# Moving an fp32 gather behind its P V, and one P V behind two score sums, in a decode attention kernel

## Chip, cores, metric

One core of a Trainium2 chip. The metric is the device time of one execution in microseconds (us), the median of several runs. The span of a profiled execution is about 1.8 us shorter than its device time.

## The reference

The kernel computes one decode step of a gated mix of two blocks, for a batch of 8.

```python
# A: cached attention. x [8,1,576], k_cache and v_cache [8,32,4096,128] bf16
q = (x @ wq).reshape(8, 1, 32, 128).transpose(0, 2, 1, 3)
p = softmax(einsum("bhqd,bhkd->bhqk", q, k_cache) * 128**-0.5)
a = einsum("bhqk,bhkd->bhqd", p, v_cache).transpose(0, 2, 1, 3).reshape(8, 1, 4096) @ wo
# B: an MLP of width 4608 on layernorm(x)
b = gelu(layernorm(x) @ w1 + b1) @ w2 + b2
g = sigmoid((x * gate_w).sum(-1, keepdims=True))
out = g * a + (1 - g) * b
```

The K and V caches are 537 MB of the 557 MB that have to be read. There is one query per head, so nothing is read twice.

## The kernel before

The work is cut into 64 groups (`NG`), each of 4 heads of one batch element: 4 MiB of K and 4 MiB of V. K and V have two buffers each. One group passes through these steps:

1. `mult`: VectorE multiplies a quarter of K by the broadcast q (bf16).
2. Sum: TensorE adds the products up, 8 matmuls with the identity.
3. `reduce`: VectorE adds the remaining 16 columns. Steps 1 to 3 run four times per group, c = 0 to 3.
4. `softmax`: the maximum on VectorE, the exponentials on ScalarE.
5. `pv`: P V on TensorE, 32 matmuls. Their result is 128x512 and holds the wanted rows in pieces.
6. `evict`: ScalarE copies it to `O_sb` (fp32, a single buffer).
7. `gather`: TensorE picks and adds the pieces, 4 fp32 matmuls, which the trace records as 8 passes.
8. `norm`: VectorE divides by the row sums, which `total` has summed over partitions.

P V of group g-1 runs within group g. All engines work from queues in the order of recording, so the place of a call in this loop is its place on TensorE. Cuts are marked "[...]".

```python
def scores(g, between):
    mult(g, 0); between(0)          # mult(g, c) also records sum c on TensorE
    mult(g, 1); between(1)
    for c in range(NCK):            # NCK = 4
        reduce(g, c)
        if c + 2 < NCK:
            mult(g, c + 2); between(c + 2)

def evict(g):    # ScalarE: O_sb <- PSUM; waits for pv(g) and for the gather of g-1
def gather(g):
    for tt in range(TQ):            # TQ = 4
        p_oz[g] = op("tensor", lambda e, tt=tt: e.matmul(
            oz_ps[:, 0:HB], lhsT=O_sb[:, tt, :], rhs=sel16[:, tt, :], start=(tt == 0), stop=(tt == TQ - 1)),
            [a_ev[g], v_norm.get(g - 1), c_sel16] if tt == 0 else ())

V_LAST = (32, 32, 16, 16, 16, 8, 8)  # load_v_pieces: the last V comes in 7 pieces of the 128 tiles
                                     # and waits, as every load_v(g), for pv(g-2), which frees its buffer
for g in range(NG):
    [...]  # load_k(g + 1), load_v(g)
    def between(c, g=g):
        if c == 0 and 2 <= g < NG - 1:
            gather(g - 2)                    # between sum 0 and sum 1
        if c == 1 and g >= 1:
            rowsum(g - 1)
            if g < NG - 1:
                if g >= 2:
                    norm(g - 2)
                total(g - 1)
        [...]  # c == 2: portions of the MLP and of the output projection
        if c == 3:
            if 1 <= g < NG - 2:
                pv(g - 1, 0, 1)
                evict(g - 1)
            if g == NG - 1:
                gather(NG - 3)
            [...]
    scores(g, between)
    [...]  # g == NG - 3: load_k(g + 2), load_v(g)
    if g + 1 < NG:
        q_of(g + 1)                          # broadcast the next q
    [...]
    softmax(g)
    if g == NG - 2:
        pv(g - 1, 0, 1)                      # P V of 61, before the sums of group 63
        evict(g - 1)
        load_v_pieces(g + 1)
last = NG - 1
norm(last - 2); pv(last - 1, 0, 1); evict(last - 1); total(last - 1); rowsum(last)
pv_turned(last, (0,))      # the last P V is turned: V is the stationary operand, 128 small matmuls
gather(last - 1); norm(last - 1)
pv_turned(last, (1,)); total(last); recip(last)
pv_turned(last, range(2, len(V_LAST))); norm_turned(last)
[...]  # the last part of the output projection, the mix with g, and the stores
```

## Time and profile before

1312.12 us, median of 3 runs (1311.38 to 1313.95).

These are lines of the page of the kernel before: the busy time of each engine with its share of the span (PE is TensorE at a matmul, PEld TensorE loading weights, DVE VectorE, ACT ScalarE, POOL GpSimd), and, in 40 equal slices of the span, the busy tenths of the DMA engines and what they moved.

```profile
span 1310.0 us, 12641 instructions
PE 870.3 (66%) x5428; PEld 416.0 (32%) x5428; DVE 870.8 (66%) x1061; ACT 204.1 (16%) x393; POOL 2.5 (0%) x13
...
DMA  9999999999999999999999999999999999999997
GB/s 401 418 432 431 432 431 431 432 432 432 432 429 431 430 430 432 425 417 432 432 431 432 430 432 431 432 430 432 431 429 431 430 432 431 431 432 432 431 418 295
```

No compute engine is busy for more than two thirds of the span, but the DMA engines are at work in all slices but the last, at about 431 GB/s. The Trainium skill, "DMA: Bandwidth & Descriptors" (Bandwidth), gives 435 GB/s as the ceiling of the fabric; the trace agrees to within 1%.

The view of waits (engine, line and tile, "<-" what it waited for, total us, times, longest) says how much slack the compute has:

```profile
DVE p L354 <- DMA KB<-in_A_k_cache_dram: 182.4, 62, 14.8
...
DVE rz L438 <- PE psb L432: 123.8, 62, 2.4
DVE s_sb L369 <- PE psb L364: 105.0, 90, 3.3
```

VectorE (DVE, line 354 is `mult`) waits 182.4 us for K, 2.9 us per group. Line 438 is the reciprocal in `norm`; it waits 2 us in each group for the gather (line 432). As there is slack in each group, that wait alone doesn't say that it costs time.

The timeline of the last 30 us (start, length, engine, line, what, count, and in brackets how long the engine sat idle before and what ended that) tells another story. L414 is P V, L364 the sums, L187 the issue of the last V, L396 the exponentials, L508 the turned P V:

```profile
1281.20 4.45 DVE L354 TENSOR_TENSOR p<-KB,q_bc 128x4096 bf16<-128x4096 bf16 x2
1284.28 3.35 PE L414 MATMUL psb<-VB,P 128*16 128x512 bf16 x32 [4.93 <-DMA VB<-in_A_v_cache_dram]
...
1287.56 3.63 PE L364 MATMUL psb<-p,ident 128*128 128x512 bf16 x16
1287.68 4.04 SPq L187 DMA_DIRECT2D VB<-in_A_v_cache_dram  x7
...
1299.16 2.34 ACT L396 ACTIVATE P<-s_sb,mD 32x128 bf16<-32x128 f32 x4 [10.88 <-DVE mD L393]
...
1301.64 0.94 PE L508 MATMUL psb<-P,VB 128*128 128x4 bf16 x32 [1.56 <-ACT P L396]
1302.45 1.03 PE L432 MATMUL psb<-sel,O_sb 128*128 128x4 f32 x8
...
1304.44 1.85 PE L508 MATMUL psb<-P,VB 128*128 128x4 bf16 x64
```

The products of group 63 are under way from 1281.20, but their sums wait on TensorE behind P V of group 61, whose V lands only at 1284.24. Once started, nothing on TensorE waits for a DMA any more: the last line has no bracket. The end of this kernel is compute.

### The profile page before, as it was taken

The page shows a single profiled execution, that of the slowest core. Times are in us where ns is not written, and L with a number is a line of the kernel's source. Part 1 is how long each engine was busy: PE and PEld are TensorE (multiplying, and loading weights), DVE is VectorE, ACT ScalarE, POOL GpSimd, SP SyncE. Part 2 cuts the span into 40 slices and gives each one's busy share as a digit, 9 for nine tenths or more (in the row PEclk, how much of TensorE's full clock was granted, in tenths as well). Part 3 has the DMA queues.
Part 4 walks back from the last instruction along what each step waited for, and adds up shares of the span by engine and source line. Part 5 has one row for each costly group of instructions (what it writes and reads, how often), then busy time and mean ns, then how long its engine had stood idle before and what let it go on. Part 6 is the DMA issues. An engine that isn't in the chain of part 4 may idle for free.

```text
span 1310.0 us, 12641 instructions
## 1 busy us (share of the span) xinstructions
PE 870.3 (66%) x5428; PEld 416.0 (32%) x5428; DVE 870.8 (66%) x1061; ACT 204.1 (16%) x393; POOL 2.5 (0%) x13
## 2 busy tenths in 40 slices
PE   3466877776647676646765855766765756766756
PEld 1133433443313333323332322333332322332323
DVE  4576676666647677647766666767676676666675
ACT  1201011111110110101011011111011011111111
POOL 0000000000000000000000000000000000000000
PEclk8778777868776888768878788878878787878888
DMA  9999999999999999999999999999999999999997
GB/s 401 418 432 431 432 431 431 432 432 432 432 429 431 430 430 432 425 417 432 432 431 432 430 432 431 432 430 432 431 429 431 430 432 431 431 432 432 431 418 295
DMA packets 25256, 557.78 MB, mean 426 GB/s; under 512 B 2529, under 2 KB 6641, under 8 KB 7537
## 3 DMA queue, kind: packets, MB, share of 16 engines
q1 hardware_dynamic: 24944, 556.95, 99.3%
q8 instruction: 42, 0.69, 0.2%
q14 instruction: 14, 0.11, 0.0%
q10 hardware_dynamic: 256, 0.03, 0.0%
HBM read 556.96 MB, written 0.01 MB: 425 GB/s over the span
## 4 chain that ended last, share of the span: by engine, by line
DMA 66%; DVE 17%; PE 16%; issue 0%; ACT 0%; SPq 0%
DMA KB<-in_A_k_cache_dram 64%; DVE p L354 14%; PE psb L364 12%; PE psb L432 3%; DVE s_sb L369 3%; DMA VB<-in_A_v_cache_dram 2%; PE psb L414 0%; PE psb L508 0%; DVE rz L438 0%; DVE OT_sb L439 0%; ACT P L396 0%; ACT L467 0%; SPq L187 0%; SPq L223 0%; PE psb L477 0%
## 5 line engine op out<-in xcount | busy, mean ns | idle before, releaser
L364 PE MATMUL psb<-p,ident 128*128 128x512 bf16 x2048 | 638.9, 469 | 415.7 <-DVE p L354 415.7
L354 DVE TENSOR_TENSOR p<-KB,q_bc 128x4096 bf16<-128x4096 bf16 x256 | 579.6, 2285 | 182.4 <-DMA KB<-in_A_k_cache_dram 182.4
L364 PEld LDWEIGHTS psb<-p,ident 128*128 128x128 bf16 x2048 | 223.5, 119 | 723.5 <-DVE p L354 449.9
L369 DVE TENSOR_REDUCE s_sb<-psb 128x32 f32<-128x512 f32 x256 | 175.7, 687 | 105.3 <-PE psb L364 105.0
L427 ACT ACTIVATE O_sb<-psb 128x512 f32<-128x512 f32 x63 | 37.6, 597 | 1030.2 <-PE psb L414 1030.2
L396 ACT ACTIVATE P<-s_sb,mD 32x128 bf16<-32x128 f32 x256 | 147.0, 574 | 18.2 <-DVE mD L393 14.4
L414 PE MATMUL psb<-VB,P 128*16 128x512 bf16 x2016 | 121.4, 383 | 4.9 <-DMA VB<-in_A_v_cache_dram 4.9
L432 PEld LDWEIGHTS psb<-sel,O_sb 128*128 128x128 f32 x504 | 99.7, 274 | 21.0 <-issue 16.2
L438 DVE RECIPROCAL rz<-psb 128x4 f32<-128x4 f32 x63 | 11.5, 182 | 123.8 <-PE psb L432 123.8
L432 PE MATMUL psb<-sel,O_sb 128*128 128x4 f32 x504 | 86.3, 294 | 0.0
L414 PEld LDWEIGHTS psb<-VB,P 128*16 128x16 bf16 x2016 | 45.0, 89 | 75.7 <-issue 27.5
L402 DVE TENSOR_REDUCE rs<-P 128x4 f32<-128x512 bf16 x64 | 43.5, 680 | 2.1 <-ACT P L396 2.1
L421 PEld LDWEIGHTS psb<-rs,ones 128*128 128x128 f32 x128 | 30.7, 241 | 15.3 <-issue 8.0
L348 ACT ACTIVATE q_bc<-psb 128x128 bf16<-128x128 f32 x64 | 17.4, 271 | 32.4 <-PE psb L346 32.4
L421 PE MATMUL psb<-rs,ones 128*128 128x4 f32 x128 | 20.9, 234 | 0.0
L452 PEld LDWEIGHTS psb<-yT_sb,RB 128*128 128x128 bf16 (+1 forms) x216 | 19.4, 165 | 3.4
L452 PE MATMUL psb<-yT_sb,RB 128*128 128x8 bf16 (+1 forms) x216 | 19.8, 227 | 0.0
L387 DVE TENSOR_REDUCE mA<-s_sb 128x1 f32<-128x128 f32 x64 | 18.3, 286 | 2.2
L389 DVE STREAM_TRANSPOSE mB<-mA 128x32 f32<-128x32 f32 x64 | 13.6, 212 | 2.2
L393 DVE STREAM_TRANSPOSE mD<-mC 128x32 f32<-128x32 f32 x64 | 13.5, 211 | 2.2
L346 PEld LDWEIGHTS psb<-Q,Sel 128*128 128x128 bf16 x64 | 6.1, 96 | 27.4 <-issue 27.2
L346 PE MATMUL psb<-Q,Sel 128*128 128x128 bf16 x64 | 14.7, 230 | 0.0
(63 smaller groups left out, 85.5 us busy)
## 6 DMA issues: line engine op xcount, KB each, us to landing
KB<-in_A_k_cache_dram SPq DMA_DIRECT2D x64, 4096.0 KB, 26.0
VB<-in_A_v_cache_dram SPq DMA_DIRECT2D x63, 4096.0 KB, 31.8
RB<-in_B_w_dram SPq DMA_DIRECT2D x1, 5184.0 KB, 43.7
RB<-in_B_w_dram SPq DMA_DIRECT2D x1, 4608.0 KB, 35.8
RB<-in_A_wo_dram SPq DMA_DIRECT2D x1, 4608.0 KB, 43.8
RB<-in_A_wq_dram SPq DMA_DIRECT2D x1, 4096.0 KB, 12.5
VB<-in_A_v_cache_dram SPq DMA_DIRECT2D x2, 1024.0 KB, 10.3
VB<-in_A_v_cache_dram SPq DMA_DIRECT2D x3, 512.0 KB, 12.9
```

Source lines behind the costliest of these rows:

```text
L346: t = op("tensor", lambda e: e.matmul(qb_ps[:, 0:DH], lhsT=Sel[:, b, :], rhs=Q4[:, hg * DH:(hg + 1) * DH], start=True, stop=True), [a_Q[hg ...
L354: v_mult[g, c] = op("vector", lambda e: e.tensor_tensor(out=p1[:, par, :, :], in0=KB[s][:, c * CT:(c + 1) * CT, :], in1=qb, op=ALU.mult), ...
L364: p_sum[g, c] = op("tensor", lambda e, r=r, n=n: e.matmul(tr_ps[par][:, :], lhsT=ident[:, :], rhs=r, start=(n == 0), stop=(n == NCH - 1)), w)
L369: v_red[g, c] = op("vector", lambda e: e.tensor_reduce(out=s_sb[:, s, c * CT:(c + 1) * CT], in_=tr_ps[par][:, :].rearrange("p (t c) -> p t ...
L387: t = op("vector", lambda e: e.tensor_reduce(out=mA[:, 0:1], in_=s_sb[:, s, :], axis=AX.X, op=ALU.max), [v_red[g, NCK - 1], c_mA])
L396: a_exp[g] = op("scalar", lambda e, h=h, q=q: e.activation(out=P[q, s, :, h], in_=s_sb[q, s, :], func=ACT.Exp, bias=mD[q, s, 0:1], scale=1.0),
L402: v_rs[g] = op("vector", lambda e: e.tensor_reduce(out=rs[:, s, :], in_=P[:, s, :, :].rearrange("p t h -> p h t"), axis=AX.X, op=ALU.add), ...
L414: p_pv[g] = op("tensor", lambda e, o=o, tq=tq: e.matmul(o, lhsT=P[:, s, tq * TQ:(tq + 1) * TQ, :].rearrange("p t h -> p (t h)"), rhs=VB[s] ...
L421: p_z[g] = op("tensor", lambda e: e.matmul(oz_ps[:, HB:2 * HB], lhsT=ones[:, :], rhs=rs[:, g % 2, :], start=True, stop=True), [v_rs[g], v_ ...
L427: a_ev[g] = op("scalar", lambda e: e.activation(out=O_sb[:].rearrange("p t d -> p (t d)"), in_=o_ps[s][:, :], func=ACT.Copy), [p_pv[g], p_ ...
L432: p_oz[g] = op("tensor", lambda e, tt=tt: e.matmul(oz_ps[:, 0:HB], lhsT=O_sb[:, tt, :], rhs=sel16[:, tt, :], start=(tt == 0), stop=(tt == ...
L452: st["p_up"] = op("tensor", lambda e, w=w, o=o, kt=kt: e.matmul(o, lhsT=w, rhs=yT_sb[:, kt, :], start=(kt == 0), stop=(kt >= NKF)), [*ld_w ...
```

## The change

The intent is to take the gather out of the chain of a group's sums. It is put where TensorE idles, behind P V and the next q broadcast. In the last group, P V of 61 is put behind the first two sums, so that they don't wait for its V.

```diff
         def between(c, g=g):
-            if c == 0 and 2 <= g < NG - 1:
-                gather(g - 2)
             if c == 1 and g >= 1:
                 rowsum(g - 1)
                 if g < NG - 1:
                     if g >= 2:
                         norm(g - 2)
                     total(g - 1)
+                else:
+                    pv(NG - 3, 0, 1)
+                    evict(NG - 3)
+                    load_v_pieces(g)
[...]
-                if g == NG - 1:
-                    gather(NG - 3)
[...]
             load_wo()
+        if 1 <= g < NG - 2:
+            gather(g - 1)
+        if g == NG - 1:
+            gather(g - 2)
         softmax(g)
-        if g == NG - 2:
-            pv(g - 1, 0, 1)
-            evict(g - 1)
-            load_v_pieces(g + 1)
     last = NG - 1
```

## The prediction

> **What bounds the kernel.** The page: span 1310.0 us, TensorE and VectorE each 66% busy, but the DMA row is 9 in 39 of 40 slices, at about 431 GB/s. The chain of waits is 66% DMA, nearly all landings of K. The Trainium skill, "DMA: Bandwidth & Descriptors" (Bandwidth), gives a fabric ceiling of 435 GB/s; this trace sits at it. In the group view VectorE waits 182.4 us for K over 62 groups: about 3 us of slack in each.
>
> Each load raises its semaphore 16 times, once per DMA engine (same page, why a DMA increments by 16). In the trace's semaphore records the last of the 16 moves by 9.71 us per 4 MiB, from 24.7 to 1304.39 us almost without a break; the first engines run up to 8.2 us ahead of it. So the slowest engine is the clock, from the first K to the last piece of V at 1304.39; then a tail of 5.6 us.
>
> **What the change does.** Nothing is added or removed; only TensorE's order moves.
> 1. The gather (4 fp32 matmuls, 8 passes, 0.8 to 1.7 us in the timeline) leaves the place between sums 0 and 1 and stands behind the next q broadcast, where TensorE idles 5 us. There it waits about 0.7 us for the eviction (0.60 us). Sums, the reciprocal that waited for it (123.8 us in all) and the first score reduction come about 1.1 us earlier per group. All of this becomes more waiting for K: gain in steady state 0.
> 2. Group 62 (VectorE-bound behind its K at 1264.8) ends about 1.05 us earlier, so group 63 starts near 1280.15, not 1281.20.
> 3. In group 63 P V of 61 (3.35 us at half clock, 1284.28 to 1287.63) no longer stands before the sums. Sum 0 starts near 1282.5 instead of 1287.56; the group's exponentials end near 1298.2 (1301.5 before).
> 4. The price: the last V's pieces wait for that P V, which now follows two sums and ends near 1289.8, so they are issued 2.2 us later (1287.68 before). Before, the first engines idled about 2.5 us for them (V of 62 landed there at 1287.86, the first piece at 1292.80), but the slowest engine had work until 1294.43 and received the first piece 2.49 us later, without a gap. Now the first engines receive it near 1295, the slowest still at about 1296.9. Last landing stays near 1304.4 (estimate from these times).
>
> **The critical path.** Before, the end was compute: the last 64 turned P V matmuls ran 1304.44 to 1306.29 without waiting, then 3.7 us to the end. After, they wait for the last piece: 1304.4 + 0.1 + 8 tiles at 29 ns = 1304.8, plus 3.7 = 1308.4. Gain about 1.5 us: 0.1%.
>
> **Predicted:** 1310.7 us (1312.12 - 1.5), 80% range 1308.8 to 1312.9. Faster by over 2%: 0.5%; within 2%: 98.5%; slower: 1%.
>
> **What would show it.** VectorE's wait for K grows from 182 to about 240 us; the reciprocal's wait for the gather falls from 124 to nearly 0; gathers sit 0.7 us behind the q broadcast; the last V is issued near 1289.8; the DMA dip at 1287 to 1290 is longer; the chain ends with a landing of V ahead of the last turned P V.
>
> **What would make it wrong.** P V of 61 later than about 1292: the slowest engine starves and the end slips by as much. The late issue costing all 16 engines alike: the end 1 to 2 us later, the gain gone. One more 1.2 us hiccup of the slowest engine. A run-to-run level (before: 1311.38 to 1313.95) that shifts as much as the effect.

## The result

1310.72 us, median of 4 runs (1310.44 to 1311.21); the kernel before, in all its runs up to then, 1313.03 us (1311.38 to 1314.13). The ratio is 0.9984, 95% interval 0.9967 to 1.0001. A ratio here is the mean time of one kernel's runs over the mean of the other's of the same rounds, so not quite the ratio of the medians. The interval touches 1; what speaks for a real gain is that all runs of the changed kernel lie close together and the profile shows where the time went.

The same lines of the page after:

```profile
span 1308.8 us, 12641 instructions
PE 843.5 (64%) x5428; PEld 384.4 (29%) x5428; DVE 869.7 (66%) x1061; ACT 204.1 (16%) x393; POOL 2.5 (0%) x13
...
DMA  9999999999999999999999999999999999999997
GB/s 398 422 431 432 431 432 431 432 431 430 434 424 432 430 431 429 428 418 432 429 431 429 431 431 431 431 432 430 432 430 431 431 431 429 432 431 432 429 420 311
```

And of the waits after:

```profile
DVE p L354 <- DMA KB<-in_A_k_cache_dram: 278.0, 62, 16.0
...
DVE s_sb L369 <- PE psb L364: 129.6, 127, 1.9
...
PE psb L432 <- ACT O_sb L427: 32.9, 61, 0.5
...
DVE rz L438 <- PE psb L432: 1.9, 1, 1.9
```

The wait of the reciprocal for the gather has gone (123.8 to 1.9 us) and the wait for K has grown by 95.6 us, 1.5 us per group. The rate of the DMA did not move. So the time that the gather's new place takes out of each group's chain turned into more waiting for K. The gather itself now waits 0.5 us for the eviction, where TensorE had nothing else to do.

The timeline after of the same stretch:

```profile
1280.30 4.45 DVE L354 TENSOR_TENSOR p<-KB,q_bc 128x4096 bf16<-128x4096 bf16 x2
...
1282.60 5.05 PE L364 MATMUL psb<-p,ident 128*128 128x512 bf16 x16 [4.15 <-DVE p L354]
...
1287.58 1.90 PE L414 MATMUL psb<-VB,P 128*16 128x512 bf16 x32
...
1289.53 3.77 SPq L187 DMA_DIRECT2D VB<-in_A_v_cache_dram  x7
...
1295.62 2.34 ACT L396 ACTIVATE P<-s_sb,mD 32x128 bf16<-32x128 f32 x4 [5.49 <-DVE mD L393]
...
1298.91 1.62 PE L432 MATMUL psb<-sel,O_sb 128*128 128x4 f32 x8
...
1303.47 1.00 PE L508 MATMUL psb<-P,VB 128*128 128x4 bf16 x24 [0.63 <-DMA VB<-in_A_v_cache_dram]
1304.72 0.38 PE L508 MATMUL psb<-P,VB 128*128 128x4 bf16 x8 [0.25 <-DMA VB<-in_A_v_cache_dram]
```

The exponentials of group 63 start 3.54 us earlier (1295.62, not 1299.16). The last V is issued 1.85 us later (1289.53, not 1287.68). The last turned P V now carries a bracket: it waits for the last pieces of V. Of the 3.5 us won, 1.2 us reach the end of the span.

Why did the later issue not cost more? A load raises its semaphore once for each of the 16 DMA engines that carry it, as the Trainium skill, "DMA: Bandwidth & Descriptors" (Why a DMA increments its semaphore by 16 and not by 1), says; the trace has the 16 times. Here are the first and the last of the 16, in us, read from the semaphore records of both traces:

```
                          before: first engine, last     after: first engine, last
V of group 61                     1278.15  1284.24              1277.87  1284.17
V of group 62                     1287.86  1294.43              1287.58  1294.68
V of group 63, issued at          1287.68                       1289.53
  piece 1 (1 MiB)                 1292.80  1296.92              1294.24  1297.14
  piece 7 (256 KB)                1300.77  1304.39              1302.09  1304.68
```

The engines are far apart. The first one had landed V of 62 by 1287.86 before and 1287.58 after, and landed piece 1 only 4.9 and 6.7 us later. Moving a piece takes about 2.5 us, as the last engine shows, so the first one stood idle for about 2.5 us before and 4.2 us after (an estimate from these times). The last engine was still at work on V of 62 and went on with piece 1 without a gap: it landed it 2.49 us later before and 2.46 us later after. These last landings set the end of the changed kernel. They come 0.3 us later than before, but 0.25 us of that is there already at V of 62, on an engine that did not have to wait for the late issue. (In a second trace of the changed kernel V of 62 is no later than before, at 1294.39, and the time is lost at piece 6, which lands 0.98 us after piece 5, not 0.62. A later section shows what costs such time.) The delay hit engines that had time. (The records do not name the engine of a landing; that the last one is the same engine from load to load is read from the even steps of the last landing.)

### The profile page after: what moved, and what is told of

The parts are those of the page before. It is cut to its first block, busy times and chain, and to the rows that moved or that the text cites. A ratio compares the mean times of both kernels' runs of the same rounds, so it can differ in the third digit from the quotient of the medians.

```text
span 1308.8 us, 12641 instructions
## 1 busy us (share of the span) xinstructions
PE 843.5 (64%) x5428; PEld 384.4 (29%) x5428; DVE 869.7 (66%) x1061; ACT 204.1 (16%) x393; POOL 2.5 (0%) x13
## 4 chain that ended last, share of the span: by engine, by line
DMA 69%; DVE 20%; PE 10%; SPq 0%; issue 0%; ACT 0%
DMA KB<-in_A_k_cache_dram 68%; DVE p L354 16%; PE psb L364 10%; DVE s_sb L369 3%; DMA VB<-in_A_v_cache_dram 1%; SPq L187 0%; PE psb L414 0%; ACT L467 0%; SPq L229 0%; DVE mA L387 0%; SPq L223 0%; PE psb L477 0%; DVE mB L389 0%; ACT O_sb L427 0%; DVE gm L390 0%
## 5 line engine op out<-in xcount | busy, mean ns | idle before, releaser
L364 PE MATMUL psb<-p,ident 128*128 128x512 bf16 x2048 | 610.9, 459 | 412.2 <-DVE p L354 411.8
L354 DVE TENSOR_TENSOR p<-KB,q_bc 128x4096 bf16<-128x4096 bf16 x256 | 579.6, 2285 | 278.0 <-DMA KB<-in_A_k_cache_dram 278.0
L364 PEld LDWEIGHTS psb<-p,ident 128*128 128x128 bf16 x2048 | 218.1, 114 | 744.5 <-DVE p L354 445.2
L432 PE MATMUL psb<-sel,O_sb 128*128 128x4 f32 x504 | 66.9, 256 | 32.9 <-ACT O_sb L427 32.9
L432 PEld LDWEIGHTS psb<-sel,O_sb 128*128 128x128 f32 x504 | 61.6, 192 | 41.3 <-ACT O_sb L427 41.2
L421 PEld LDWEIGHTS psb<-rs,ones 128*128 128x128 f32 x128 | 24.4, 192 | 9.3 <-issue 0.4
L390 DVE TENSOR_REDUCE gm<-mB 128x1 f32<-128x32 f32 x64 | 11.9, 186 | 2.2
```

The source lines that it names most:

```text
L354: v_mult[g, c] = op("vector", lambda e: e.tensor_tensor(out=p1[:, par, :, :], in0=KB[s][:, c * CT:(c + 1) * CT, :], in1=qb, op=ALU.mult), ...
L364: p_sum[g, c] = op("tensor", lambda e, r=r, n=n: e.matmul(tr_ps[par][:, :], lhsT=ident[:, :], rhs=r, start=(n == 0), stop=(n == NCH - 1)), w)
L421: p_z[g] = op("tensor", lambda e: e.matmul(oz_ps[:, HB:2 * HB], lhsT=ones[:, :], rhs=rs[:, g % 2, :], start=True, stop=True), [v_rs[g], v_ ...
L432: p_oz[g] = op("tensor", lambda e, tt=tt: e.matmul(oz_ps[:, 0:HB], lhsT=O_sb[:, tt, :], rhs=sel16[:, tt, :], start=(tt == 0), stop=(tt == ...
```

## The experiments

Twelve kernels ran, each beside the kernel before on the same chip. One interval of ratios is 0.0025 wide or wider, more than most of the effects looked for, so the verdicts rest on spans and times in the traces, and the ratios are given with them.

### The changed kernel again

No edit.

> The changed kernel once more, as the yardstick of this chip. Theory T (the gain is in the tail alone: compute of group 63 comes forward by about 3.5 us and the end is then set by the last landing of V): ratio 0.9985 to 0.9995, span near 1308.8. Rival S (the gather's place gives the time in all groups): the same, so this run does not tell them apart.

Measured: 1310.74 us (1310.59 to 1311.04, 5 runs), before on this chip 1311.91 (1310.37 to 1314.81, 9 runs), ratio 0.9990 (0.9977 to 1.0002); span 1308.9. The last landing was at 1304.75. The result repeats. The runs of the kernel before are spread over 4.4 us, those of the changed one over 0.5 us; the fastest of the kernel before is faster than any of these.

### The gather alone

```diff
 # against the changed kernel
-                else:
-                    pv(NG - 3, 0, 1)
-                    evict(NG - 3)
-                    load_v_pieces(g)
[...]
         softmax(g)
+        if g == NG - 2:
+            pv(g - 1, 0, 1)
+            evict(g - 1)
+            load_v_pieces(g + 1)
```

> The gather behind P V, but P V of group 61 still at the end of group 62. T: P V of 61 waits for its V (about 1284.2) and holds up the sums of group 63 as before, exponentials of 63 end near 1301.5, the last turned P V runs without a wait, span 1310.0, ratio 0.9995 to 1.0005: no gain, though the waiting for K grows from 182 to about 278 us. S: all of the gain, span 1308.8, ratio 0.9985.

Measured: 1312.24 us (1311.67 to 1313.82), ratio 0.9998 (0.9985 to 1.0012); the profiled run had 1313.82, span 1312.0. VectorE's wait for K is 278.6 us, so all of the slack is there, and none of the gain. From the timeline of this kernel:

```profile
1284.13 3.59 PE L414 MATMUL psb<-VB,P 128*16 128x512 bf16 x32 [5.78 <-DMA VB<-in_A_v_cache_dram]
...
1287.65 4.55 PE L364 MATMUL psb<-p,ident 128*128 128x512 bf16 x16
...
1306.48 1.85 PE L508 MATMUL psb<-P,VB 128*128 128x4 bf16 x64
```

The sums wait for P V of 61 again, and the last turned P V runs without waiting, although the last V had landed at 1304.36. That the span is 2 us above the one before fits an end that compute sets: TensorE was granted 0.55 of its clock from 1286 to 1290 here and 0.84 in the trace of the kernel before; the first two sums of group 63 took 4.55 us here and 3.63 there, and the gather of group 62 took 1.85 us here and 1.03 us there. The Trainium skill, "TensorE: Matmul & The Clock Gate" (Part 1), says that the clock is halved after idle windows and that the window runs freely, so that its phase differs from run to run; both traces show shares between 0.5 and 1 here. That this makes the whole 4.4 us of spread of the kernel before was not tested. The clock is no rival for the gain: its mean over the whole run rose from 0.804 to 0.818 with the change, but it is 0.818 in this kernel too, which gained nothing.

### P V of group 61 alone

```diff
 # against the kernel before
                     total(g - 1)
+                else:
+                    pv(NG - 3, 0, 1)
+                    evict(NG - 3)
+                    load_v_pieces(g)
[...]
-        if g == NG - 2:
-            pv(g - 1, 0, 1)
-            evict(g - 1)
-            load_v_pieces(g + 1)
```

> The gathers stay between sum 0 and sum 1, only P V of group 61 follows two sums of group 63. T: group 63 starts near 1281.2 as before, its sums no longer wait for V of 61, exponentials end near 1299, the last V is issued near 1290.4, last landing near 1304.7 and the end is set by it: span 1308.8 to 1309.2, ratio 0.9985 to 0.9995, nearly all of the gain. S: no gain, or a loss by the later issue: ratio 1.000 or above.

Measured: 1310.75 us (1310.70 to 1311.88), ratio 0.9991 (0.9979 to 1.0004); span 1309.3. The wait for K is 180.2 us, as before. So most of the gain is in this half of the change (0.7 of the 1.2 us by the spans, and three of the five times are as those of the changed kernel), and the gather's move alone gives none: the traces speak for theory T and against S, although the intervals of the two ratios overlap. Two parts of the expectation failed. Group 63 started at 1282.40 and its two sums took 6.26 us, at 0.50 of the clock from 1286 to 1290, so that the issue came at 1292.85. And TensorE does not wait for the last landing here: the last turned P V has no bracket. The lines:

```profile
1284.71 6.26 PE L364 MATMUL psb<-p,ident 128*128 128x512 bf16 x16 [4.16 <-DVE p L354]
...
1290.90 1.90 PE L414 MATMUL psb<-VB,P 128*16 128x512 bf16 x32
...
1292.85 3.45 SPq L187 DMA_DIRECT2D VB<-in_A_v_cache_dram  x7
...
1303.59 1.99 PE L508 MATMUL psb<-P,VB 128*128 128x4 bf16 x64
```

When the pieces reached the engines, every engine had run dry: the last one had landed V of 62 at 1294.17, and piece 1 landed on the first engine at 1297.09 and on the last at 1297.52. The last landing was at 1305.16, 0.5 us later than in the changed kernel, and compute and the landing end nearly together. With the gathers moved as well, the issue came between 1289.4 and 1289.9 in the four traces with P V in this place and single gathers, clear of this edge; with four gathers (below) it came at 1292.7. So moving the gathers is worth something to the end after all: room for the late issue.

### P V of group 61 after one, three and four sums

```diff
 # against the changed kernel; N = 0, 2 or 3 where the changed kernel has 1
-                else:
-                    pv(NG - 3, 0, 1)
-                    evict(NG - 3)
-                    load_v_pieces(g)
[...]
+            if c == N and g == NG - 1:
+                pv(NG - 3, 0, 1)
+                evict(NG - 3)
+                load_v_pieces(g)
```

> As the changed kernel, but P V of 61 follows one sum of group 63, not two: the last V is issued about 1.9 us earlier, near 1288, the compute stays 2 to 3 us ahead of before. T: the last landing is set by the slowest engine, which has work until 1294.7, so the earlier issue is worth nothing: last landing 1304.4 to 1304.7, span 1308.5 to 1308.9. Rival D (the later issue delays the last landing directly, by the 0.3 us seen or more): last landing and span 0.3 to 1 us earlier than the changed kernel.

> P V of 61 after three sums of group 63: the last V is issued near 1292.5. T: from the first issue to the last landing are about 12.3 us once every engine has run dry (1292.85 to 1305.2 in the run with P V alone moved), and the slowest engine runs dry near 1292; so last landing 1304.9 to 1305.3, span 1309.0 to 1309.5, 0.2 to 0.6 us worse than the changed kernel: the edge of the slack. Rival E (any delay of the issue shows one to one in the end): about 3 us worse, span near 1312.

> P V of 61 after all four sums of group 63: issue near 1295.3. T: past the edge the delay shows one to one: all 16 engines idle, first piece on all of them near 1299.6, last landing 1295.3 + 12.3 = 1307.6, span 1311.6 to 1312.2, which gives away all that the change gained. Rival F (the place of P V does not matter to the end): span 1308.8.

Measured, by the time of the issue, with the two kernels above (us):

```
P V of 61 after        issue    V 63 lands, last   span     device time, ratio
1 sum                  1288.10  1304.96            1309.0   1310.81, 0.9989 (0.9976 to 1.0001)
2 sums (the change)    1289.53  1304.68            1308.8   1310.72, 0.9984 (0.9967 to 1.0001)
2 sums, old gather     1292.85  1305.16            1309.3   1310.75, 0.9991 (0.9979 to 1.0004)
3 sums                 1293.04  1306.73            1310.9   1312.58, 0.9998 (0.9984 to 1.0013)
4 sums                 1295.71  1309.31            1313.4   1315.28, 1.0019 (1.0004 to 1.0034)
```

Between 1288.1 and 1289.5 the time of the issue does not show; an earlier issue landed no earlier, against rival D. From 1289.53 to 1292.85 the issue moves by 3.32 us and the last landing by 0.48, against rival E. From three to four sums the issue moves by 2.67 us and the last landing by 2.58, against rival F. In the last three rows piece 1 lands on the last engine 4.67 to 4.71 us after the issue, which is one to one. No run issued between 1289.9 and 1292.7, so the edge is an estimate: piece 1 reaches an engine some 2.2 us after the issue (4.7 less the 2.5 that it takes), and the last engine is done with V of 62 at 1294.2 to 1295.0, so it lies between 1292 and 1293, near where the expectation put it. But three and four sums came out at 1310.9 and 1313.4, where 1309.0 to 1309.5 and 1311.6 to 1312.2 were expected. The semaphore records show what was missed. With three sums, piece 5 landed on fifteen engines from 1303.55 to 1304.08, and on one at 1305.45. With four sums, piece 4 landed on fifteen from 1305.04 to 1305.41, and on one at 1306.79. One engine lost about 1.4 us at once, and all that follows waits for it. The DMA records have one packet of 16 KB of the queue "instruction" at 1303.2 and at 1304.2 in these two runs. These are fetches of instructions, TensorE's by their number: 42 packets for 10856 recorded matmuls and weight loads, and two fewer when 504 of these went (below). That the packet and the late landing are of the same engine is inferred from the times; the records do not name the engine.

### Four gathers instead of one

```diff
 # against the kernel before, and against the changed kernel
     def gather(g):
-        for tt in range(TQ):
+        for tt in list(range(TQ)) * (4 if g < 56 else 1):
```

> The kernel before with every gather up to group 55 done four times over (same result), between sum 0 and sum 1. Three more gathers are 3.2 to 5.1 us of TensorE in the chain of a group, whose slack is 182.4 / 62 = 2.9 us. T: the slack is used up in most groups: 0.3 to 2.2 us per group, 15 to 120 us longer, ratio 1.01 to 1.09; the wait for K nearly gone. Rival: with the DMA as the bound it costs nothing, ratio 1.000.

> The changed kernel with the same four gathers behind P V, where TensorE is idle for 5 us while the next K lands. T: 4 x 1.05 us fit into the idle time, no group gets longer: span within 1.5 us of the changed kernel (1308.8 to 1310.5; the added instructions have to be fetched and a fetch of 16 KB takes a DMA engine 1.1 us). That is what the new place is worth: slack, not time. Rival: as much longer as the kernel before with four gathers.

Measured: before with four gathers 1368.95 us, ratio 1.0428 (1.0380 to 1.0476); changed with four gathers 1312.86 us, ratio 1.0006 (0.9989 to 1.0022). Of the waits, in the first one:

```profile
DVE rz L438 <- PE psb L432: 280.2, 62, 7.5
...
DVE p L354 <- DMA KB<-in_A_k_cache_dram: 30.5, 5, 14.9
```

and in the second:

```profile
DVE p L354 <- DMA KB<-in_A_k_cache_dram: 280.8, 62, 15.8
...
DVE rz L438 <- PE psb L432: 1.3, 1, 1.3
```

Between the sums, three more gathers used up the slack in all but five groups, and the kernel became 56 us longer. Behind P V the same work vanished into TensorE's idle time, and the wait for K is as in the changed kernel. This is what the gather's new place is worth: room, not time.

But the second is 2.0 us above the changed kernel by its span (1310.8), a little more than expected. It has 53 instruction packets, not 42, and K of 62 landed on the last engine at 1267.29, not 1264.74. The next paragraphs follow this up.

### What slows the slowest engine

The trace lists the instruction packets. Every eighth of them fits the times at which the last engine's landings are late (steps between landings of 4 MiB loads are 9.71 us, the late ones in this table 10.5 to 11.3):

```
changed kernel   packets 1, 9, 17, ...   52.7  275.1  507.5  762.6  1022.8  1289.0
                 late landings at               283.1  510.7  767.1  1030.9  1294.7
four gathers     packets 1, 9, 17, ...   50.1  230.3  427.5  613.4  798.3   999.0  1203.3
                 late landings at               234.8  433.2  621.5  807.6  1003.5  1209.0
```

A packet took about 1.1 us on its engine. The kernel before has the same pattern (packets 9, 17, 25, 33 and 41, late landings at 282.9, 510.6, 766.8, 1030.6 and 1294.4). Smaller late steps follow other packets: in the changed kernel 10.0 to 10.1 us after packets 5, 21, 29 and 37, as if another engine had overtaken the last. One of 10.1 us at 1255 fits no packet of 16 KB; it comes 9 us after a packet of 8 KB of a second instruction queue, and its cause stays open. The weight loads have larger steps because they are larger. The Trainium skill, "Runtime: NRT & Kernel Launch" (Instruction fetch mechanics), says that the instructions are refilled in blocks of 16 KiB by DMA, which the trace agrees with (42 packets of 16,384 bytes), and calls the cost "mostly hidden". For TensorE it may be: the view of waits names no fetch. For a DMA engine that sets the time, it isn't. To test it, fewer instructions:

```diff
 # against the changed kernel
-    sel16 = sb("sel16", [128, TQ, HB], F32)
+    sel16 = sb("sel16", [128, TQ, HB], BF16)
[...]
-    O_sb = sb("O_sb", [128, TQ, DH], F32)
+    O_sb = sb("O_sb", [128, TQ, DH], BF16)
[...]  # and the leave to build with low precision
```

> The changed kernel with the gathered outputs and the selection matrix in bf16 instead of fp32: half of the gather's 504 recorded matmul passes and weight loads go, about 504 instructions of 12641. Theory I (every eighth instruction packet of 16 KB is fetched by the same DMA engine, and the slowest engine is the one that got six of the 42): about 40 packets instead of 42, the slowest engine gets five, the late +0.8 us step of its V landing at 1294 goes, last landing 1303.9 to 1304.3 instead of 1304.7, span 1308.0 to 1308.5, ratio 0.998 to 0.9985. Theory N (the fetches do not matter to the end): last landing 1304.7, span 1308.8 to 1308.9, as the changed kernel.

Measured: 1310.43 us (1309.90 to 1311.28), ratio 0.9985 (0.9972 to 0.9999); span 1308.1. The gather has four passes instead of eight, and from the page:

```profile
span 1308.1 us, 12137 instructions
...
q8 instruction: 40, 0.66, 0.2%
```

where the changed kernel has

```profile
q8 instruction: 42, 0.69, 0.2%
```

The late step at 1294 has gone (V of 62 lands on the last engine at 1294.00, not 1294.68), the last landing is at 1304.01, and the end follows, 0.7 us earlier than in the changed kernel. This is theory I, by the numbers. The comparison holds across chips: up to V of 61 the last landing of this trace (1284.29) is within 0.3 us of that in the trace of the kernel before and in three of the changed kernel (one with a cut gather, below), and with V of 62 all four have a late step, of 10.2 to 10.5 us, while this one has 9.71. It is one trace, though. Its interval alone, of all that ran, lies below 1, and it is the fastest kernel by median; but two of its five runs were at 1311.1 and 1311.3, so that it beats the changed kernel in the trace, not clearly in the times. It gives up precision in the gathered sums, and passed the comparison with the reference. The next section shows that this comparison is not sharp.

### One gather cut short in the tail

```diff
 # against the kernel before, and against the changed kernel
     def gather(g):
-        for tt in range(TQ):
+        n = 1 if g == NG - 2 else TQ
+        for tt in range(n):
[...]
-            start=(tt == 0), stop=(tt == TQ - 1)),
+            start=(tt == 0), stop=(tt == n - 1)),
```

> The kernel before with one matmul of the four in the gather of group 62, which stands between the turned P V pieces of the tail (wrong result for that group, on purpose). T: the end of the kernel before is compute, so the time saved on TensorE (three quarters of 1.0 to 1.85 us) shows in the end: 0.7 to 1.4 us less until the last landing binds; ratio 0.9989 to 0.9996. If the end were the landing of V, nothing would show.

> The same cut in the changed kernel (wrong result for that group, on purpose). T: the end of the changed kernel is the last landing of V, so the saving is lost in a longer wait for it: span 1308.8 to 1309.0, the same as the changed kernel within 0.2 us. If compute still set the end: 0.7 to 1.4 us less.

Measured: in the kernel before 1311.43 us (1310.27 to 1312.74) beside 1311.85, ratio 0.9995 (0.9982 to 1.0008), span 1309.4: less, as expected, but inconclusive, as the interval holds 1. In the changed kernel 1310.49 us, ratio 0.9988, span 1308.7: last landing 1304.61, 0.07 us earlier than in the changed kernel, end 0.15 us earlier. There TensorE was done with the gather early, and waited longer for the pieces of V: the saving did not reach the end. Both kernels, wrong in one group of 64, passed the comparison: its tolerance doesn't see the outputs of one group.

### An uneven load

```diff
 # against the changed kernel, in load_v; shortened
-        t = op("sync", lambda e: e.dma_start(VB[s][:, :, :], src), ...)
+        if g == NG - 2: one transfer each for partitions (0, 96), (96, 104), (104, 112), (112, 120), (120, 128)
```

> The changed kernel with the load of V of group 62 cut by partitions: 96 partitions in one transfer over all 16 engines, the other 32 in four transfers of 8 partitions, which the Trainium skill (DMA: Bandwidth & Descriptors, on how many engines a DMA uses) says go to the lowest-numbered 8 engines. Nine engines lag by 5 to 7 us at that point. If the leading engines are the lowest-numbered ones, they take 10 partitions instead of 8, the lagging ones 6: the last landing of V of 62 comes 2.4 us earlier on these, the last piece lands near 1302.5 to 1303, span 1306.5 to 1307.5: faster than both kernels. If the lagging ones are the lowest-numbered, the reverse: last landing near 1307.2, span 1311 to 1312. Either shows that the slowest engine, not the mean rate, sets the end.

Measured: 1335.24 us, ratio 1.0177 (1.0163 to 1.0191), span 1334.8. Neither expectation: 24 us longer. From the windows of this kernel (stretch and length, busy time of PE, PEld, DVE, ACT and POOL, granted clock, DMA share, GB/s):

```profile
1264.00:1274.00 10.00, 5.63 (x20) 2.47 (x21) 8.65 (x8) 0.00 (x0) 0.00 (x0) 0.68 1.00 429
1280.00:1290.00 10.00, 6.03 (x16) 2.08 (x16) 9.07 (x9) 2.30 (x4) 0.00 (x0) 0.66 1.04 197
1300.00:1310.00 10.00, 2.02 (x14) 1.44 (x12) 2.93 (x10) 2.29 (x4) 0.00 (x0) 0.73 0.89 164
```

The DMA engines are as busy as ever, but they move less than half: a packet of 32 KB took 2.8 us on the mean from 1280 to 1290, where it took 1.22 us up to 1275. The slow packets last as long as the uneven load is in flight, until 1320.89. The pieces of the last V, whose transfers had their usual shape, shared the engines with it and were slow too (0.61 us for a packet of 8 KB from 1305 to 1315); once it had landed they took their usual times (0.31 us from 1320 on, 0.33 in the changed kernel). The semaphore records show 48 landings for the five transfers, 16 for the large one and so eight for each small one, as the expectation took it. An engine that carries six partitions of the large transfer and one of each small one, not eight of one, writes other partitions than usual, perhaps together with another engine; no run tested that. Whether the leading engines are the lowest-numbered ones stays open as well.

## Why the prediction was right

- **The bound.** Right. DMA at 431 GB/s in steady state before and after, and slack in each group. Moving the gather alone gave a ratio of 0.9998.
- **Step 1, the gather.** Right in kind: the wait of the reciprocal went from 123.8 to 1.9 us, the saving became a wait for K. Mis-sized: 0.9 us per group were forecast for the wait for K (182 to 240), 1.5 us measured (182.4 to 278.0). The gather's passes alone took 86.3 us in 63 groups before, 1.4 us per group. As none of it reaches the end, the error does not show in the time.
- **Steps 2 and 3, the last group.** Group 63 started at 1280.30 (forecast 1280.15), sum 0 at 1282.60 (1282.5), the exponentials ended at 1297.96 (1298.2), the last V was issued at 1289.53 (1289.8).
- **Step 4, the price.** The last landing was forecast near 1304.4 and came at 1304.68, with the slowest engine at work without a gap. That the first engines would receive piece 1 near 1295 was 0.8 us too late (1294.24), without effect. The series over the place of P V confirms the mechanism: flat up to an issue at 1289.5, and one to one from 1292.85 on. It also supports the first item of what would make it wrong: with P V of 61 ending near 1292.8 the last landing slips by 0.5 us, and after all four sums the gain is gone. With three sums the gain is gone too, but 1.4 us of that loss is the instruction packet.
- **The end.** Forecast 1308.4, span 1308.8; device time 1310.7 forecast and 1310.72 measured. That the device times agree so closely is luck: with 1.8 us between span and device time, a span of 1308.4 would have been 1310.2, but the forecast took its gain from the median of 1312.12, which lies 0.3 us above the profiled run (1311.82), and the span came 0.4 us late. The difference of the spans is the 0.3 us of the landing, and the last eight tiles, 0.38 us and not 0.23. The gain by device time was forecast as 1.5 us from 1312.12; by the median of all runs of the kernel before it is 2.3 us, which says more of that kernel's spread than of the change.

The hiccups of 1.2 us of the slowest engine were named in the prediction as a risk, without a cause. The runs point to one: every eighth instruction packet. The times fit in the traces of both kernels, and one experiment with fewer packets came out as this cause demands.

## What to carry to other kernels

Where every transfer waits its turn, time taken out of compute in the steady state becomes waiting; look for gains where the last transfer ends, and ask there whether the last work waits for a landing or runs without a wait. Here a later issue cost nothing as long as the slowest DMA engine still had work, and its full delay after: look at all 16 landing times of a load, not at the rate. And once the end is a landing, the DMA time of the instructions themselves is in the account.

## What the Trainium skill lacked or had wrong

- "Runtime: NRT & Kernel Launch" (Instruction fetch mechanics) calls the cost of a block boundary mostly hidden. In a kernel bound by DMA it is not: each 16 KB packet held one DMA engine for about 1.1 us, every eighth was followed by a late landing on the last engine, and removing 2 of 42 packets brought the last landing from 1304.68 to 1304.01 us.
- "DMA: Bandwidth & Descriptors" gives one rate for each engine and says that the engines finish independently; of two it says that they are usually slower, which it lays to transfers issued by GpSimd. It does not say that the engines of a queue issued by SyncE drift apart over a long stream, nor by how much: the landings of one load were 0.4 us apart at 25 us and 8.2 us at 1255 us, and the last engine sets the time.
- The same page (Why a DMA increments its semaphore by 16 and not by 1) tells how many engines a transfer uses, but not what an uneven cut costs: 96 + 4 x 8 partitions instead of 128 brought the rate from 429 to 197 GB/s, and to 164 GB/s from 1300 to 1310, where it shared the engines with the regular transfers behind it.
